# Identity by DMA, another order of the first loads, two weight loads ahead of the first gather, and one list operand on ScalarE

## The chip, the core and the metric

The kernel runs on one core of a Trainium2 chip. The metric is the device time of one execution in microseconds. The core has five engines that run side by side and in order, each through its own list of instructions: TensorE (PE, with its weight loads as PEld), VectorE (DVE), ScalarE (ACT), GpSimd (POOL) and SyncE (SP). DMA transfers are issued by an engine into a queue of its own and carried out by 16 DMA engines that all queues share. An instruction that has to wait for another engine, or for a transfer, waits at the head of its engine's list, and all behind it waits too.

## The reference, cut to what matters

```python
# attention in chunks of 64 tokens: q, k, v are (8, 8, 576, 64)
scores = scale * q_c @ k_c.T              # each chunk of 64 against itself
attn = exp(scores - max) ; attn /= sum + 1e-9
x = (attn @ v_c)  ->  (4608, 512)

# mixture of experts, 8 experts, a capacity of 576 tokens each
logits = x @ w_gate
for idx in argsort(-logits.flatten()):    # greedy: best logit first
    tok, e = idx // 8, idx % 8
    if not assigned[tok] and counts[e] < 576: assign
x[mask_e] = max(x[mask_e] @ w1[e], 0) @ w2[e]     # 512 -> 1024 -> 512

# a second block on all tokens
h = max(x @ m1, x @ m2, x @ m3)           # 512 -> 768
out = h @ w_out                           # 768 -> 512
```

All arrays are float32. The routing needs exact logits, and each expert gets exactly 576 tokens.

## The kernel before, in words

The program is written as one list for each engine; the order on an engine is the order of the code. There are three parts.

**Attention.** The 4608 tokens go in nine units of 512, each unit in four steps, 36 steps in all. A unit's k and q come with `load_qk` (lines 46 to 56), its v with `load_v` (lines 58 to 66: sixteen DMAs of 64 KB a unit, four for each of its four parts). PE turns k and q by transposes against an identity matrix (line 95), DVE and ACT copy the result out of PSUM into the block tiles kb and qT (`evac`, line 107), then come the scores (line 116), the softmax on DVE and ACT, a second transposing and the product with v (line 166). DVE scales the result into x (line 173, three buffers), and SP stores x to a DRAM array xd (line 175). The tiles kb and vb hold zeros in half of their blocks; these are set once by memsets at the start (lines 73 to 76). SP issues every load and store of this part; unit 0 and unit 1 are loaded ahead of the loop. The one exception is the gate weights wg, which ACT loads (line 83), after a memset of the tile on DVE (line 82).

The identity is made in `Router.__init__` (lines 278 to 284) by `make_identity`: POOL sets the tile to zero and then writes ones on the diagonal with an affine select.

**Routing and experts.** `Router.round` (lines 389 to 531) picks for one expert the 576 tokens it gets. It is a generator: the first round runs alone, the rounds for the later experts are stepped through while the expert before computes. At its end it makes the list of tokens. A comparison on DVE gives the tile `at` (line 503, 128 x 720), two multiplications give the two halves of an operand, `tok[:, 0]` by column (line 504) and `tok[:, 1]` by row (line 505), and 36 small matmuls add them up (line 511). DVE casts the sums into `ids` (line 514), PE folds them (line 520), and DVE casts the fold into the index `idx` (line 522).

With the index POOL gathers the expert's rows of xd in five indirect DMAs (line 614; 128 tokens each, 64 in the last). PE transposes the rows (line 637), ACT and DVE part them into a high and a low half (lines 639, 640), and the expert runs as two products (line 796 with ReLU at lines 805 and 813, then line 825); each operand is kept as a high and a low half, and every product is made of such halves. The copy of the result is ACT's (line 832), and ACT stores it too (line 833).

The expert weights come in chunks of 512 KB. `issue` (line 574) lets SP load one into one of four raw buffers; `split` (line 586) parts it, first a cast on ACT (line 594, the high half), then a subtraction on DVE (line 595, the low half). A counter sets the pace: `pump` (line 715) is called between the matmuls, steps the routing of the next expert, the weights of the last block (lines 677 to 709, with an `ACTIVATE` into ct at line 688) and, every second time, `pump_loads` (line 598), which splits the oldest chunk when it is old enough and issues another load. In the first round the loop at lines 728 to 731 issues loads while the list is made. After the gather's issue PE runs twelve matmuls without use (`warm`, line 732), two chunks are split, three row tiles are transposed, and SP stores one element of the last gathered tile to a DRAM cell `tick` (line 746): SP thus waits for the end of the gather before it issues more weights.

**The last block.** Lines 876 to 905 run over nine blocks of 512 tokens; nothing in it is touched.

What sets the order of issue on SP: a DMA's completion is counted on one of eight counters, given out in turn to the DMAs of SP and ACT in the order of the code, and a DMA is issued only after the one before it on the same counter has landed.

## Time and profile before

| | |
|---|---|
| median of three runs | 1318.49 us (1316.15 to 1322.0) |
| the profiled execution | 1317.84 us, its span in the trace 1316.1 us |
| PE busy | 1245.3 us (95%) |
| PE's weight loads | 1085.4 us (82%) |
| DVE busy | 663.9 us (50%) |
| ACT busy | 397.4 us (30%) |
| POOL busy | 108.5 us (8%) |

Busy is the time in which an engine carried out an instruction; time in which it waited or issued a DMA does not count. In the rows further down, a line like `L505 DVE ... aoh<-aoh,row` tells the line of the code, the engine, and what was made out of what, by the names of the tiles. Tiles that share a buffer share the first name it had: `aoh` stands for the operands of the list too, `rp` for the small results in PSUM, `pT` for the transposes of q and k, `raw` and `chunk` for an expert's weights before and after the parting. A name with a `q` behind an engine, such as SPq, is the engine's issuing side. The idle time in brackets is that of the engine just ahead of the instruction, with what ended it. PEclk is the mean clock that the chip granted TensorE, 1.00 for 2.4 GHz and 0.50 for 1.2 GHz.

### The profile page before, as it was taken

To read this page: it belongs to the slowest core of one execution; us is meant where nothing else is said; L and a number is where in the kernel's file an instruction comes from. 1 tells how busy PE (TensorE), PEld (TensorE's weight loads), DVE (VectorE), ACT (ScalarE), POOL (GpSimd) and SP (SyncE) were. 2 spreads that over 40 slices of the span, in tenths; PEclk is the share of its full clock that TensorE was granted. 3 is DMA by queue.
4 is the path that set the end of the run, shared out by engine and by line. 5 is a ranking of instruction groups with operands and counts; after the bars stand their busy time and mean duration, and the time that the engine had idled before them with its cause. 6 is when DMAs were issued, how large, how long until landed. Compare 5 with 4: busy or idle time off the path is not lost.

```text
span 1316.1 us, 20997 instructions
## 1 busy us (share of the span) xinstructions
PE 1245.3 (95%) x8669; PEld 1085.4 (82%) x8669; DVE 663.9 (50%) x1332; ACT 397.4 (30%) x621; POOL 108.5 (8%) x171
## 2 busy tenths in 40 slices
PE   5999975998999999999999999999999999999997
PEld 4877854988888988999999888888888888888885
DVE  5777876888787888795422422222222222222221
ACT  4877831332432323343323212121212121212110
POOL 6000001011010110110000000000000000000001
PEclk9999985999999999999999999999999999999998
DMA  8888724264553544567314101010101010100000
GB/s 196 215 223 226 222 76 132 65 228 138 156 173 108 166 139 134 183 216 236 104 65 171 60 17 49 17 48 16 48 20 45 25 41 24 40 24 9 24 9 32
DMA packets 147458, 135.60 MB, mean 103 GB/s; under 512 B 45731, under 2 KB 122531, under 8 KB 147363
## 3 DMA queue, kind: packets, MB, share of 16 engines
q1 hardware_dynamic: 136402, 105.93, 27.3%
q0 software_dynamic: 5824, 18.88, 4.2%
q10 hardware_dynamic: 5136, 9.46, 2.0%
q8 instruction: 68, 1.11, 0.4%
q14 instruction: 28, 0.22, 0.1%
HBM read 99.63 MB, written 34.60 MB: 102 GB/s over the span
## 4 chain that ended last, share of the span: by engine, by line
PE 39%; issue 35%; DVE 13%; DMA 6%; POOL 2%; ACT 2%; SPq 2%; POOLq 0%; ACTq 0%; DVEq 0%
PE acc L825 12%; PE acc L796 10%; PE acc L876 5%; DMA xd<-x 4%; PE pc L876 3%; DVE chunk L595 2%; PE po L899 2%; POOL out_dram L905 2%; DVE hlo L813 1%; PE pX L166 1%; SPq L64 1%; PE pS L116 1%; PE pT L95 1%; DVE ge L417 1%; PE pxt L637 1%
## 5 line engine op out<-in xcount | busy, mean ns | idle before, releaser
L825 PE MATMUL acc<-hhi,chunk 128*128 128x288 f32 x1024 | 214.7, 303 | 0.0
L796 PE MATMUL acc<-xhi,chunk 128*128 128x288 f32 x1024 | 210.9, 305 | 1.3 <-ACT xhi L639 0.7
L796 PEld LDWEIGHTS acc<-xhi,chunk 128*128 128x128 f32 x1024 | 162.8, 191 | 3.9 <-DVE hlo L813 1.3
L825 PEld LDWEIGHTS acc<-hhi,chunk 128*128 128x128 f32 x1024 | 164.1, 190 | 1.0
L885 DVE TENSOR_TENSOR tb<-ta,acc 128x512 f32<-128x512 f32 x54 | 37.1, 688 | 235.1 <-ACT ta L883 235.1
L825 PE MATMUL acc<-hlo,chunk 128*128 128x288 f32 x512 | 151.6, 296 | 0.1
L876 PE MATMUL acc<-yxhi,chunk 128*128 128x512 f32 x480 | 147.8, 389 | 0.0
L796 PE MATMUL acc<-xlo,chunk 128*128 128x288 f32 x512 | 144.4, 297 | 0.0
L876 PE MATMUL acc<-yodd,chunk 128*128 128x512 f32 x576 | 134.5, 389 | 0.0
L876 PEld LDWEIGHTS acc<-yodd,chunk 128*128 128x128 f32 x576 | 108.1, 188 | 22.5
L595 DVE TENSOR_TENSOR chunk<-raw,chunk 128x1024 fp32r<-128x1024 f32 x75 | 90.9, 1219 | 33.2 <-ACT chunk L594 33.2
L876 PEld LDWEIGHTS acc<-yxhi,chunk 128*128 128x128 f32 x480 | 90.0, 188 | 18.7
L825 PEld LDWEIGHTS acc<-hlo,chunk 128*128 128x128 f32 x512 | 96.9, 189 | 0.3 <-DVE hlo L813 0.3
L796 PEld LDWEIGHTS acc<-xlo,chunk 128*128 128x128 f32 x512 | 94.8, 190 | 0.0
L883 ACT COPY ta<-acc 128x512 f32<-128x512 f32 x54 | 31.7, 587 | 206.0 <-PE acc L876 203.9
L876 PE MATMUL acc<-yxlo,chunk 128*128 128x512 f32 x240 | 93.4, 389 | 0.0
L905 POOL DMA_INDIRECT out_dram<-ot,ia x36 | 34.7, 964 | 671.0 <-DVE ot L903 618.2
L805 ACT ACTIVATE hhi<-acc 128x576 fp32r<-128x576 f32 x64 | 41.8, 652 | 152.5 <-PE acc L796 152.5
L594 ACT CAST chunk<-raw 128x1024 fp32r<-128x1024 f32 x75 | 76.8, 1045 | 33.8 <-DMA raw<-in_moe_w_dram 26.1
L899 PE MATMUL po<-chunk,hm 128*128 128x512 f32 x324 | 79.3, 389 | 0.0
L886 DVE TENSOR_TENSOR tb<-tb,pc 128x512 f32<-128x512 f32 x54 | 37.1, 687 | 73.4 <-PE pc L876 73.4
L876 PE MATMUL pc<-yxhi,chunk 128*128 128x512 f32 x240 | 73.9, 389 | 0.0
(197 smaller groups left out, 1827.5 us busy)
## 6 DMA issues: line engine op xcount, KB each, us to landing
raw<-in_moe_w_dram SPq DMA_DIRECT2D x64, 512.0 KB, 5.3
vb<-in_v_dram SPq DMA_DIRECT2D x144, 64.0 KB, 3.6
xd<-x SPq DMA_DIRECT2D x36, 256.0 KB, 4.2
c<-in_moe_w_dram SPq DMA_DIRECT2D x36, 256.0 KB, 4.1
yd<-ys ACTq DMA_DIRECT2D x32, 288.0 KB, 3.5
yraw<-yd SPq DMA_DIRECT2D x9, 1024.0 KB, 5.0
m<-ct SPq DMA_DIRECT2D x36, 128.0 KB, 1.9
raw<-m SPq DMA_DIRECT2D x9, 512.0 KB, 3.7
```

Source lines behind the costliest of these rows:

```text
L64: nc.sync.dma_start(t[s * 64:(s + 1) * 64, j, :, s, :], bass.AP(tensor=v.tensor, offset=v.offset + b * H * S * D + s * S * D + c * 64 * D, ...
L594: nc.scalar.copy(hi, raw)
L595: nc.vector.tensor_tensor(lo, raw, hi.bitcast(F32), op=OP.subtract)
L796: nc.tensor.matmul(acc[:, hf, :288], w[a][:, dc, o:o + 128], x[:, dc, tk], start=n == 0, stop=n == 11)
L805: nc.scalar.activation(hv, acc[:, :, :288], AF.Relu)
L825: nc.tensor.matmul(acc[:, hf, :288], w[a][:, f, :], x[:, f, tk], start=n == 0, stop=n == 23)
L876: nc.tensor.matmul(ps, w[a][:, dc, o:o + 128], x[:, dc], start=n == 0, stop=n == 11)
L883: nc.scalar.copy(ta, pab[:, 0])
L885: nc.vector.tensor_tensor(tb, ta, pab[:, 1], op=OP.max)
L886: nc.vector.tensor_tensor(tb, tb, pc, op=OP.max)
L899: nc.tensor.matmul(po, h[:, x, t * 128:t * 128 + 128], w[a][:, f % 2], start=n == 0, stop=n == 17)
L905: st = nc.gpsimd.indirect_dma_start(out=out, out_offset=bass.IndirectOffsetOnAxis(ap=ia[:, 4 * b + t:4 * b + t + 1], axis=0), in_=ot, in_o ...
```

## The change

Four things are changed.

1. The identity. DVE sets the tile to zero and its column 0 to one. ACT stores this tile (128 x 128, 64 KB) to a DRAM array `unit` and reads it back with a pitch of 127 elements between rows and not 128, so that the one of row p comes to stand p places to the right. POOL no longer takes part.
2. The start. The memset and the load of wg are written ahead of the other memsets; the memsets of the first vb tile go from POOL to DVE; and unit 0's v and unit 1's k and q are loaded in turns (v part 0, k and q part 0 of unit 1, v parts 1 and 2, k and q part 1 of unit 1, v part 3) and no longer all of v first.
3. The list operand `tok[:, 1]` is made on ACT, as a copy with a scale for each partition, and no longer on DVE.
4. Two weight loads and not four are issued ahead of the first gather.

```diff
--- before.py
+++ after.py
@@ -4,7 +4,6 @@
 import concourse.tile as tile
 from concourse import mybir
 from concourse._compat import with_exitstack
-from concourse.masks import make_identity
 from concourse.bass_isa import ReduceOp
 
 F32 = mybir.dt.float32
@@ -68,19 +67,21 @@
 
     load_qk(0, 0)
     load_qk(0, 1)
+    wg = C.tile([128, 4, 32], F32, name="wg")
+    nc.vector.memset(wg, 0.0)
+    nc.scalar.dma_start(wg[:, :, :8], wg_in.rearrange("(a p) e -> p a e", p=128))
     VB = [C.tile([128, 8, 4, 2, 64], F32, name="vb%d" % i) for i in range(3)]
     KB = [C.tile([128, 8, 4, 2, 64], F32, name="kb%d" % i) for i in range(2)]
-    for t, eng in ((KB[0], nc.vector), (KB[1], nc.gpsimd), (VB[0], nc.gpsimd), (VB[1], nc.gpsimd),
+    for t, eng in ((KB[0], nc.vector), (VB[0], nc.vector), (KB[1], nc.gpsimd), (VB[1], nc.gpsimd),
                    (VB[2], nc.gpsimd)):
         eng.memset(t[0:64, :, :, 1, :], 0.0)
         eng.memset(t[64:128, :, :, 0, :], 0.0)
-    for part in range(4):
-        load_v(0, part)
+    load_v(0, 0)
     load_qk(1, 0)
+    load_v(0, 1)
+    load_v(0, 2)
     load_qk(1, 1)
-    wg = C.tile([128, 4, 32], F32, name="wg")
-    nc.vector.memset(wg, 0.0)
-    nc.scalar.dma_start(wg[:, :, :8], wg_in.rearrange("(a p) e -> p a e", p=128))
+    load_v(0, 3)
 
     def trans(nm, u, n):
 
@@ -275,13 +276,17 @@
 
 
 
-    def __init__(s, ctx, tc, mark):
+    def __init__(s, ctx, tc, mark, scratch):
         s.tc, s.mark = tc, mark
         nc = s.nc = tc.nc
         C = s.C = ctx.enter_context(tc.tile_pool(name="rc", bufs=1))
         s.L = C.tile([128, G, E], F32, name="L")
         s.ident = C.tile([128, 128], F32, name="ident")
-        make_identity(nc, s.ident)
+
+        nc.vector.memset(s.ident, 0.0)
+        nc.vector.memset(s.ident[:, 0:1], 1.0)
+        nc.scalar.dma_start(scratch, s.ident)
+        nc.scalar.dma_start(s.ident, bass.AP(tensor=scratch.tensor, offset=scratch.offset, ap=[[127, 128], [1, 128]]))
 
     def consts(s, tmp):
         nc, C = s.nc, s.C
@@ -502,7 +507,7 @@
 
         nc.vector.tensor_tensor(at, bb(qi, 20), s.i20[:, None, :].to_broadcast([128, G, 20]), op=OP.is_equal)
         nc.vector.tensor_tensor(tok[:, 0], at, s.col, op=OP.mult)
-        nc.vector.tensor_scalar(tok[:, 1], at, s.row, None, op0=OP.mult)
+        nc.scalar.activation(tok[:, 1], at, AF.Copy, scale=s.row)
         yield 3
         mark("r.list")
         pi = PS.tile([128, 2, 5, 4], F32, name="rp", tag="rp", bufs=2)
@@ -541,7 +546,8 @@
     yd = dram.tile([DM, NT], F32, name="yd")
     tick = dram.tile([1, 1], F32, name="tick")
     ms = [dram.tile([DM, F2], F32, name="m%d" % i) for i in range(3)] + [dram.tile([F2, DM], F32, name="mo")]
-    rt = Router(ctx, tc, mark)
+    unit = dram.tile([128, 128], F32, name="unit")
+    rt = Router(ctx, tc, mark, unit)
     with ExitStack() as c2:
         consts = c2.enter_context(tc.tile_pool(name="tmp", bufs=1))
         rt.consts(consts)
@@ -727,7 +733,7 @@
 
     rt.begin()
     for _ in rt.round(0, PS, expert):
-        if state["issued"] < 4:
+        if state["issued"] < 2:
             issue()
     def warm(n):
 
@@ -742,7 +748,6 @@
     split()
     for i in range(3):
         x_tr(0, xg, i)
-
     nc.sync.dma_start(tick, xg[4][0:1, 0:1])
 
     NB = NT // 512
```

On ACT, the first instructions of the program: before, the load of wg, the table load and the copies of the transposes (pT, out of PSUM).

```order
L947 UNCONDITIONAL_BRANCH [waits barrier_Pool_Activation_PE_DVE_SP_release]
L83 DMA wg<-in_moe_w_gate_dram 128x4x8 [waits DVE_49]
L107 ACT_TABLE_LOAD
L107 COPY kb_167<-pT 64x2x8x32 [waits PE_49]
L107 COPY qT<-pT 64x512 [waits PE_49]
```

```order
L952 UNCONDITIONAL_BRANCH [waits barrier_Pool_Activation_PE_DVE_SP_release]
L288 DMA unit<-ident 128x128 [waits DVE_49]
L289 DMA ident<-unit 128x128 [waits DMAHW1_49]
L72 DMA wg<-in_moe_w_gate_dram 128x4x8 [waits DVE_49]
L108 ACT_TABLE_LOAD
L108 COPY kb_171<-pT 64x2x8x32 [waits PE_49]
```

The store and the read of the identity now stand ahead of wg; the read waits for the store's landing (DMAHW1 is its counter), and wg and the copies stand behind that.

On SP, the first v loads of unit 0 and what follows them (DMAHW0 to DMAHW7 are the eight counters; before, wg's is DMAHW3; in the changed kernel the store of the identity has DMAHW1, its read DMAHW3 and wg DMAHW5). Before:

```order
L64 DMA vb_164<-in_v_dram 64x4x64 x3
L64 DMA vb_164<-in_v_dram 64x4x64 [waits DMAHW0_49]
L64 DMA vb_164<-in_v_dram 64x4x64 [waits DMAHW1_49]
L64 DMA vb_164<-in_v_dram 64x4x64 [waits DMAHW2_49]
L64 DMA vb_164<-in_v_dram 64x4x64 [waits DMAHW3_49]
L64 DMA vb_164<-in_v_dram 64x4x64 [waits DMAHW4_49]
```

```order
L63 DMA vb_168<-in_v_dram 64x4x64
L63 DMA vb_168<-in_v_dram 64x4x64 [waits DMAHW0_49]
L63 DMA vb_168<-in_v_dram 64x4x64 [waits DMAHW1_49]
L63 DMA vb_168<-in_v_dram 64x4x64 [waits DMAHW2_49]
L52 DMA ink<-in_k_dram 16x4x256 [waits DMAHW3_49]
L52 DMA ink<-in_k_dram 112x4x256 [waits DMAHW4_49]
L52 DMA inq<-in_q_dram 16x4x256 [waits DMAHW5_49]
L52 DMA inq<-in_q_dram 112x4x256 [waits DMAHW6_49]
L63 DMA vb_168<-in_v_dram 64x4x64 [waits DMAHW7_49]
```

After four v loads, and not sixteen, stand four loads of k and q of unit 1, the first of which waits for the read of the identity.

On SP, at the first gather (raw is a buffer of weights, tick the store that waits for the gathered tile xg). Before:

```order
L566 TENSOR_LOAD ei_141
L566 ISA x2
L581 ISA
L581 DMA raw_2999<-in_moe_w_dram 128x4x256
L581 ISA
L581 DMA raw_3016<-in_moe_w_dram 128x4x256
L581 ISA
L581 DMA raw_3021<-in_moe_w_dram 128x4x256
L581 ISA
L581 DMA raw_3062<-in_moe_w_dram 128x4x256
L746 DMA tick<-xg 1x1
```

```order
L572 TENSOR_LOAD ei_142
L572 ISA x2
L587 ISA
L587 DMA raw_3000<-in_moe_w_dram 128x4x256
L587 ISA
L587 DMA raw_3017<-in_moe_w_dram 128x4x256
L751 DMA tick<-xg 1x1
L587 ISA
L587 DMA raw_3163<-in_moe_w_dram 128x4x256
L587 ISA
L587 DMA raw_3177<-in_moe_w_dram 128x4x256
```

The third and the fourth load now stand behind tick, and so behind the end of the gather.

On ACT, at the list of round 5, which runs while the expert before it computes (aoh is the list operand, xhi the high half of gathered rows, ct a step of the last block's weights, ys and yd the copy and the store of a result). Before:

```order
L639 CAST xhi<-pxt 128x4x64
L688 ACTIVATE ct<-c_6117 128x512
L594 CAST chunk<-raw_6214 128x1024
L832 COPY ys<-acc 128x576
L833 DMA yd<-ys 128x576
L594 CAST chunk<-raw_6331 128x1024
```

```order
L645 CAST xhi<-pxt 128x4x64
L510 ACTIVATE aoh<-aoh,row 128x720
L694 ACTIVATE ct<-c_6118 128x512
L600 CAST chunk<-raw_6215 128x1024
L837 COPY ys<-acc 128x576
L838 DMA yd<-ys 128x576
L600 CAST chunk<-raw_6332 128x1024
```

The new step stands ahead of a ct step and of the cast of a chunk.

## Rows read from the trace of the kernel before

**Rows 1.** Windows: stretch, us, busy PE PEld DVE ACT POOL, clock, DMA share, GB/s.

```profile
600.00:1309.00 709.00, 707.07 (x3490) 604.43 (x3488) 191.14 (x267) 136.71 (x217) 37.90 (x73) 1.00 0.14 48
```

**Rows 2.** Timeline of the first 30 us: start, duration, instruction, idle time before it.

```profile
1.23 1.76 DVE L75 MEMSET kb<- 64x2048 f32 x1 [1.23 <-PEq L936]
...
5.49 0.43 ACTq L83 DMA_DIRECT2D wg<-in_moe_w_gate_dram  x1
...
10.27 0.28 POOL masks.py:199 TENSOR_SCALAR_AFFINE_SELECT ident<-ident 128x128 f32<-128x128 f32 x1 [9.32 <-issue]
...
10.60 1.12 PE L95 MATMUL pT<-ident,ink 128*128 128x128 f32 x4 [10.60 <-DMA vb<-in_v_dram]
...
12.41 0.69 DVE L107 COPY kb<-pT 64x512 f32<-64x512 f32 x1 [6.95 <-ACT kb L107]
```

**Rows 3.** SP's second k load; packets in 0:9.3, in 9.3:10.3; landings: wg, ink, vb.

```profile
1.79 0.51 SPq L53 DMA_DIRECT2D ink<-in_k_dram  x1
...
q1 hardware_dynamic: 2877, 2.28, 78.9%
...
q10 hardware_dynamic: 528, 0.02, 31.3%
...
wg<-in_moe_w_gate_dram ACTq DMA_DIRECT2D x1, 16.0 KB, 5.8
...
DMA to landing us min/median/max: 4.0/5.0/5.9
...
DMA to landing us min/median/max: 2.3/2.4/2.7
```

**Rows 4.** Timeline of SP's issues and DVE's first x; duration of a v issue (ns).

```profile
2.89 14.91 SPq L64 DMA_DIRECT2D vb<-in_v_dram  x16
...
29.84 0.69 DVE L173 TENSOR_TENSOR x<-pX,rc 128x512 f32<-128x512 f32 x1
...
36.69 0.42 SPq L175 DMA_DIRECT2D xd<-x  x1
...
L64 SPq DMA_DIRECT2D vb<-in_v_dram x16: 595/615/738, 2.9 to 17.2; - x16
```

**Rows 5.** SP's waits in 0:20 and 20:32: in total us, times, longest.

```profile
SPq L64 <- DMA wg<-in_moe_w_gate_dram: 2.9, 1, 2.9
...
SPq L64 <- DMA inq<-in_q_dram: 1.8, 2, 1.1
SPq L53 <- DMA ink<-in_k_dram: 0.8, 1, 0.8
```

**Rows 6.** The first gather's issues (ns, first and last start), landings, first expert matmul.

```profile
L614 POOL DMA_INDIRECT xg<-xd,idx x5: 912/947/1427, 213.0 to 218.8; - x5
...
DMA to landing us min/median/max: 3.2/3.9/5.9
...
222.41 1.81 PE L796 MATMUL acc<-xhi,chunk 128*128 128x288 f32 x6 [0.67 <-ACT xhi L639]
```

**Rows 7.** Windows after the first expert matmul and at round 6's list.

```profile
226.00:228.00 2.00, 2.00 (x12) 2.00 (x12) 1.93 (x5) 0.10 (x1) 0.00 (x0) 0.64 0.69 208
520.00:525.00 5.00, 5.00 (x45) 4.74 (x40) 4.79 (x14) 0.00 (x0) 0.00 (x0) 0.66 0.52 156
```

**Rows 8.** Line 505 over all rounds: ns min/median/max, first and last start.

```profile
L505 DVE TENSOR_SCALAR aoh<-aoh,row x8: 399/400/401, 210.7 to 539.7; 128x720 bf16<-128x720 bf16 x8
```

**Rows 9.** Timeline at round 5's list; its last row is round 6's list.

```profile
468.51 1.04 ACT L594 CAST chunk<-raw 128x1024 fp32r<-128x1024 f32 x1
...
471.91 0.53 DVE L504 TENSOR_TENSOR aoh<-aoh,col 128x720 bf16<-128x720 bf16 x1
...
472.68 1.22 DVE L595 TENSOR_TENSOR chunk<-raw,chunk 128x1024 fp32r<-128x1024 f32 x1
...
474.47 0.21 PE L520 MATMUL rp<-ids,lev 128*32 128x5 f16 x8
...
519.45 0.74 PE L511 MATMUL rp<-aoh 128*32 128x40 bf16 x36 [1.58 <-DVE aoh L505]
```

## The prediction

> **What bounds the kernel now.** I read the windows by stage first, then the timeline of the first 30 us, SP's own waits, the first gather, and last the timeline round one of the list steps. The kernel is a row of stages, and only what is late next in each stage counts.
>
> At the very start PE waits for the identity: POOL makes it at 10.27 and the first transposes start at 10.60; DVE's first copy follows at 12.41, because PE's second buffer waits for it [rows 2]. From then on the attention does not follow PE but SP, which issues every load and store. It needs 14.91 us for the sixteen v loads, and the store of the first x tile leaves at 36.69 although DVE had made the tile at 29.84 [rows 4]. SP is then behind for good, and x has three buffers, so DVE soon waits for SP's stores to land. What counts in this stage is when SP gets through its list, not when PE starts. SP's own waits name what holds it: 2.9 us for the gate weights, which ACT issues, and 1.8 + 0.8 us for the second unit's q and k [rows 5].
>
> At the first gather the chain is serial: the list, the gather on POOL, transposes, and the first expert matmul at 222.41 [rows 6]. Up to about 600 us PE and DVE work in step and wait for each other; from 600 on PE is busy 707 of 709 us [rows 1]. A loss of PE time before 600 therefore stays in the time.
>
> **The change, part by part.** The sum is made against the profiled run's 1317.84 us (span 1316.1, and 1.7 around it); the median of the three runs, 1318.49, is 0.65 above that.
>
> *The start.* The identity now needs two DMAs of 64 KB one after the other, both from ACT, whose queue stands still between them. DVE can fill the tile from 1.23 on, with two memsets of about 0.2 us, so the write is issued at about 1.6. Its price is read from the one ACT load of this stage: wg was issued at 5.49 [rows 2], its queue moved no packet up to 9.3 while SP's queue moved 2877, its 528 packets all went in 9.3 to 10.3, and it landed 5.8 us after issue [rows 3]. A DMA from ACT thus stood behind what SP had issued before it. The two k loads of the first unit land 4.0 and 5.9 us after their issue, the second, issued at 1.79, at 7.7 [rows 3]. The write is issued just ahead of that one and stands behind the first half of k and q alone, so it lands near 6.5; the read stands behind the rest of the first loads and two or three v loads, which as wg did clear after 10, and lands near 10.5. That is where POOL's identity was ready: PE gains nothing (0.1). Bounded from the other side, without a queue each costs the 2.3 us of an uncrowded v load [rows 3]: 1.6 + 2 x 2.3 = 6.2. PE could then start at 6.3, but DVE, with the two memsets of VB[0] added, does four memsets of 1.76 us [rows 2] and is free at about 9.2 and not before; against 12.41 this is at most 3.2 us.
>
> The Trainium skill says something else of this queue (*DMA: Bandwidth & Descriptors*, Queues, rings and completion order): each DMA engine takes turns between the queues that have work, packet by packet, so ACT's small DMAs would not stand behind SP's. The row on wg speaks against it here. By the page the start would be worth the 3.2 us, and the rival below would be the case.
>
> *SP's list.* Every issue on SP waits for the DMA eight places before it, and unit, ident and wg take three of these places. Four v loads are out when SP stops for the read of ident at 10.5 (before: six, and a stop for wg until 11.3). Twenty issues are left up to the loop: 12 of v at 0.65 (0.615 [rows 4] and a small gap) and 8 of q and k at 0.52 (0.51 [rows 3]), 12.0 us. They end at 22.5; before it was 14.91 + 2.89 = 17.8 [rows 4] and eight issues more, 22.0. So 0.5 us later. In exchange, half of the second unit's q and k (1 MB of 2) leaves in the quiet stretch at 10 to 13 us, and not in one burst at 18 to 22, behind which SP stood for 1.8 + 0.8 = 2.6 us [rows 5]. I take that wait as gone: 0.5 - 2.6 = **-2.1 us**. Bounds: +0.5 if the waits come back later, and -4.7 if ACT's DMAs do not queue (SP would be through at about 19.9: -2.1, and the same -2.6). Compute has the slack for it: it was 6.9 us ahead at the first store. The earlier VB[0] on DVE hides ahead of 12.41, POOL is done earlier with the others, and ACT's table load ends long before its first copy; these cost nothing as long as PE does not start before 9.
>
> *The gather.* Four weight loads of 512 KB leave ahead of it; POOL's five pieces start from 213.0 to 218.8, land 5.9 us (first) to 3.2 us (last) after issue, and take 1.43 us to issue at worst against 0.91 [rows 6]. With two loads the queue is empty by about 213, so the first piece should land in the 3.2 us of the last: at 216.2 and not 218.9, the others about every 1.25 us (the median issue of 0.95 and a gap of 0.3, by the five starts). Not all 2.7 us arrive: the third tile is then bound by POOL's pace (218.7), its transposes and copy end at 220.5, and the first expert matmul starts there and not at 222.41: **-1.9 us**. The other two loads now stand behind tick, which waits for the last piece (about 221), so they land near 225 to 227; their splits stand one step later on ACT and DVE and come at about 238, so nothing waits for them: 0, at most +0.5. What is open is the clock. In 226 to 228 the grant is 0.64 on the mean [rows 7], that is, it rises from 1.2 to 2.4 GHz in there, some 5 us after the first expert matmul, with an idle stretch of PE ahead of the transposes. If the closed gap lets it rise right away, the 5 us at half clock are done in half: -2.5 more.
>
> *The list operand.* Each of eight rounds takes 0.40 us off DVE [rows 8] and puts the same tile on ACT, where a cast of 1024 columns takes 1.04 us [rows 9]; 720 columns are 0.73 of that by columns, and I take 0.78. ACT can start when L503 ends and is done 0.8 us later; on DVE the pair L504 and L505 (0.53 and 0.40 us) took about 0.9 [rows 8, 9]. The list matmuls start 0.1 us earlier at most, where ACT is free. But ACT runs in order, and the new step waits for DVE. Whatever stands behind it on ACT waits as well. In round 5 that is a ct step and the cast of a chunk. The cast ran at 468.51, 3.4 us ahead of L503's end (L504 starts at 471.91) [rows 9]. Now it comes after list (to 472.69) and ct (to 473.3) and ends at 474.2. DVE's second half of that split, which started at 472.68 [rows 9], starts at 474.25, and behind it on DVE stands ids, for which PE's fold at 474.47 [rows 9] waits: ids comes at 475.6, PE stops for 1.1 us, and everything behind it. The same reading gives 0.4 in round 4, 0.5 in round 6, 1.2 in round 7; in rounds 1 to 3 no split stands between, and 0.1 each is won. 3.2 - 0.3 = **+2.9 us**, bounds -0.3 (the casts are not waited for) and +6.3 (clock, below). The 0.40 us that DVE is spared each round does not count further, as its next wait for PE takes it up.
>
> Sum: -2.1 - 1.9 + 2.9 = -1.1, 1317.84 - 1.1 = **1316.7 us**.
>
> **The rivals.**
> (a) *ACT's DMAs take turns with SP's.* The identity lands near 6.3, wg near 8, and SP is through early: -4.7 in place of -2.1, so -3.7, 1314.1 us. For it: the trace shows ACT's queue in this stage with one DMA only. Against it: that one stood for 3.8 us [rows 2, 3].
> (b) *The list operand on ACT hurts nobody*, because the splits of rounds 4 to 7 have slack that I don't see: -0.3 for +2.9, so -4.3, 1313.5 us. Against it: DVE and PE stand back to back there [rows 9].
> (c) *The clock rises with the closed gap at the gather*: -4.4 for -1.9, so -3.6, 1314.2 us.
> (d) *Slower: the stall on ACT costs the clock too.* In round 6 PE stood 1.58 us ahead of the list [rows 9], and 520 to 525 has a mean grant of 0.66 [rows 7]. With 1.1 to 1.2 us more of standing in rounds 5 and 7, the grant could fall twice; such a fall cost half of some 3.4 us there (0.34 of 5 us at 0.50 is 1.7 us of work). 2 x 1.7 = 3.4 more: +2.3, 1320.1 us. It decides once PE's stop in these rounds is longer than the one of round 6.
> (e) *SP's list gains nothing* (the burst's waits come back, or ident lands after 12): +0.5 for -2.1: +1.5, 1319.3 us.
>
> **How the numbers follow.** Forecast 0.30, (a) 0.18, (b) 0.17, (c) 0.10, (d) 0.13, (e) 0.12. The cases are not exclusive: (a) with (b), or (b) with (c), gives -6.8 or -6.9, 1311.0, and (d) with (e) +4.9, 1322.7. The range reaches from the first of these to 1321.5, which leaves out less than 2 in 10. About 0.5% (6.6 us) is what a measurement of this kernel can tell from no change. Only two of the good cases together reach it: faster 0.14. On the bad side (d), (e) and a worse gather would all have to come: slower 0.03. Same 0.83.
>
> **What would show it.** Right, if the first transposes start between 10 and 11 us and the read of ident lands just before; if SP has no wait over 0.5 us between 22 and 32 us and the first x store leaves near 34.5; if the first piece of the gather lands 3.2 us after its issue and the first expert matmul follows the gather's issue by 7.5 us (before 9.4); if in rounds 5 and 7 ACT's cast of a chunk comes after the new step, and PE's fold waits for ids by about 1 us. Wrong, if PE starts before 9 us (a), if the fold starts on time (b), if the grant is 1.0 before 222 us (c), or if short stretches at half clock follow rounds 5 and 7 (d).

## The result, and the profile after

The changed kernel takes 1332.84 us (median of six runs, 1328.22 to 1335.68) against 1318.0 us (six runs of the kernel before, 1315.97 to 1322.0): a ratio of 1.0107, with a 95% interval of 1.0081 to 1.0133. It is 14.8 us slower by the medians, where I had forecast 1316.7 us and no difference that can be measured. The ratio is not the quotient of the two medians, which is 1.0113; by the ratio the difference is 14.1 us. The profiled execution took 1335.68 us with a span of 1333.9, the longest of the six, so it shows some 3 us more than the median.

To see where the time went I set the same DVE instruction of both traces side by side, all through the program, and took the difference of their starts. The first column is the time in the kernel before; positive means that the changed kernel is late.

| time in before, us | what stands there | changed kernel late by, us |
|---|---|---|
| 26 | attention, unit 1 begins | -1.9 |
| 46 | attention | +0.1 |
| 205 | first list | +0.7 |
| 222.4 | first expert matmul | 0.0 |
| 241 | first expert, fifth part of its first product | -1.7 |
| 247 | 6 us on | +3.4 |
| 257.5 | | +6.8 |
| 347 | expert 2 | +8.7 |
| 475 | list of round 5 | +10.9 |
| 545 | list of round 7 | +15.6 |
| 600 to the end | | +17.8 |

From 600 us on nothing changes any more. The window that answers to [rows 1], 17.8 us later, is the same to a tenth; the second row is the stretch behind the first loss, the third the one behind round 5's list (columns as in [rows 1]: length, busy time of PE, PEld, DVE, ACT, POOL, then the granted clock).

```profile
617.80:1326.80 709.00, 707.10 (x3490) 604.47 (x3488) 191.16 (x267) 136.69 (x217) 37.72 (x71) 1.00 0.14 48
250.00:256.90 6.90, 6.33 (x29) 6.02 (x29) 4.04 (x11) 0.65 (x1) 0.00 (x0) 0.51 0.01 2
485.60:489.00 3.40, 3.40 (x15) 3.40 (x15) 3.11 (x11) 0.34 (x1) 2.30 (x3) 0.50 0.71 236
```

**The start.** The timeline of the changed kernel (start, duration, engine and line), answering to [rows 2, 4]:

```profile
1.16 0.41 ACTq L288 DMA_DIRECT2D unit<-ident  x1
5.07 0.34 ACTq L289 DMA_DIRECT2D ident<-unit  x1
...
8.32 1.76 DVE L78 MEMSET vb<- 64x2048 f32 x1 [0.47 <-issue]
...
11.12 1.08 PE L96 MATMUL pT<-ident,ink 128*128 128x128 f32 x4 [11.12 <-DMA vb<-in_v_dram]
...
35.93 0.42 SPq L176 DMA_DIRECT2D xd<-x  x1
```

And SP's waits in 0 to 20 us and in 20 to 32 us, answering to [rows 5] (engine, line, what it waited for: us in total, times, longest):

```profile
SPq L52 <- DMA ident<-unit: 3.8, 1, 3.8
...
SPq L63 <- DMA inq<-in_q_dram: 0.9, 1, 0.9
```

The identity is there at 11 us, not earlier than POOL had it (10.55). DVE is through with its memsets at 10.08 us, where the prediction's bound had 9.2. SP stands 3.8 us for the identity's read, and in return the wait of 2.6 us for the second unit's q and k is down to 0.9.

**The first gather**, answering to [rows 6]: POOL's issues with their landings, and the first expert matmul in PE's timeline.

```profile
L620 POOL DMA_INDIRECT xg<-xd,idx x5: 915/947/1424, 214.0 to 219.8; - x5
...
DMA to landing us min/median/max: 3.1/3.3/3.7
```

```profile
222.41 1.81 PE L801 MATMUL acc<-xhi,chunk 128*128 128x288 f32 x6 [0.68 <-ACT xhi L645]
```

The pieces land sooner after their issue, 3.7 us at most where it was 5.9; but the gather begins 1.0 us later (0.7 us of this from the attention, 0.3 from the list), and the first expert matmul comes at 222.41 in both kernels.

**The first loss, 240 to 257 us.** ACT, DVE and PE of the changed kernel, one after the other:

```profile
239.62 1.98 ACT L600 CAST chunk<-raw 128x1024 fp32r<-128x1024 f32 x2
243.56 0.65 ACT L810 ACTIVATE hhi<-acc 128x576 fp32r<-128x576 f32 x1 [1.96 <-PE acc L801]
247.57 0.66 ACT L694 ACTIVATE ct<-c 128x512 f32<-128x512 f32 x1 [3.35 <-DMA c<-in_moe_w_dram]
248.13 1.03 ACT L600 CAST chunk<-raw 128x1024 fp32r<-128x1024 f32 x1
...
249.19 1.23 DVE L601 TENSOR_TENSOR chunk<-raw,chunk 128x1024 fp32r<-128x1024 f32 x1 [3.36 <-ACT chunk L600]
250.33 0.18 DVE L439 TENSOR_TENSOR cs<-rp,same 128x32 f16<-128x32 f32 x1
...
250.57 0.25 PE L444 MATMUL rp<-cs,lev 128*32 128x8 f16 x4 [4.35 <-DVE cs L439]
```

The same place in the kernel before, ACT and PE:

```profile
240.21 1.98 ACT L594 CAST chunk<-raw 128x1024 fp32r<-128x1024 f32 x2
244.51 0.65 ACT L805 ACTIVATE hhi<-acc 128x576 fp32r<-128x576 f32 x1 [2.32 <-PE acc L796]
247.18 0.66 ACT L688 ACTIVATE ct<-c 128x512 f32<-128x512 f32 x1 [2.02 <-DMA c<-in_moe_w_dram]
...
247.17 0.24 PE L439 MATMUL rp<-cs,lev 128*32 128x8 f16 x4
```

In both kernels ACT comes to a ct step (a step of the last block's weights) and waits for its load c, 2.02 us before and 3.35 us after. In the kernel before the four casts of this stretch, those of the third to the sixth chunk, are done by then, and nobody waits for ACT. In the changed kernel the two loads behind tick have put every split one step later; the fourth cast, that of the sixth chunk, stands behind the ct step, DVE waits 3.36 us for it, cs (a small step of the next expert's routing) waits behind it on DVE, and PE waits 4.35 us for cs. Then the granted clock stands at 0.51 for 6.9 us (the second window above).

**The later losses.** Round 5's list in the changed kernel, ACT, DVE and PE, answering to [rows 9]:

```profile
481.55 0.89 ACT L510 ACTIVATE aoh<-aoh,row 128x720 bf16<-128x720 bf16 x1 [3.87 <-DVE aoh L508]
482.35 0.68 ACT L694 ACTIVATE ct<-c 128x512 f32<-128x512 f32 x1
482.94 1.03 ACT L600 CAST chunk<-raw 128x1024 fp32r<-128x1024 f32 x1
...
484.00 1.23 DVE L601 TENSOR_TENSOR chunk<-raw,chunk 128x1024 fp32r<-128x1024 f32 x1 [1.91 <-ACT chunk L600]
485.14 0.19 DVE L519 CAST ids<-rp 128x40 f16<-128x40 f32 x1
...
485.39 0.22 PE L525 MATMUL rp<-ids,lev 128*32 128x5 f16 x8 [1.17 <-DVE ids L519]
```

This is the order that I had worked out: list operand, ct step, cast, and behind it DVE's subtraction and ids, for which PE's fold waits 1.17 us. In rounds 4, 5, 6 and 7 PE waits 0.60, 1.17, 0.43 and 1.18 us there, 3.4 in all. At rounds 5, 6 and 7 the clock falls to half: the third window above and these two, 13.6 us in all.

```profile
533.30:540.10 6.80, 6.37 (x35) 6.09 (x34) 6.05 (x18) 1.05 (x3) 0.00 (x0) 0.50 0.32 96
557.20:560.60 3.40, 3.18 (x20) 3.16 (x20) 3.26 (x9) 0.78 (x1) 0.00 (x0) 0.51 0.24 87
```

The kernel before has one such stretch there, at round 6:

```profile
521.00:524.40 3.40, 3.40 (x23) 3.22 (x22) 3.23 (x11) 0.00 (x0) 0.00 (x0) 0.50 0.45 133
```

Not every fall belongs to a stop that the edits made. The changed kernel's trace has two more of 3.4 us, from 328.5 and 349.0 us, with none of these stops ahead of them, and the trace of a kernel without the new list operand (start_alone below) has such a fall at 307.6 us too.

### The profile page after: what moved, and what is told of

Read it like the earlier page. It is cut to its first block, busy times and chain, and to the rows that moved or that the text cites. A ratio compares the mean times of both kernels' runs of the same rounds, so it can differ in the third digit from the quotient of the medians.

```text
span 1333.9 us, 21005 instructions
## 1 busy us (share of the span) xinstructions
PE 1253.2 (94%) x8669; PEld 1093.1 (82%) x8669; DVE 666.0 (50%) x1328; ACT 403.6 (30%) x629; POOL 104.3 (8%) x167
## 4 chain that ended last, share of the span: by engine, by line
PE 38%; issue 34%; DVE 12%; DMA 8%; ACT 3%; POOL 3%; SPq 1%; POOLq 0%; ACTq 0%; DVEq 0%
PE acc L830 11%; PE acc L801 9%; PE acc L881 5%; DMA xd<-x 3%; PE pc L881 3%; DVE chunk L601 3%; PE po L904 2%; POOL out_dram L910 2%; PE pX L167 2%; PE pT L96 1%; DMA c<-in_moe_w_dram 1%; PE pS L117 1%; DVE hlo L818 1%; DMA vb<-in_v_dram 1%; DVE ge L422 1%
## 5 line engine op out<-in xcount | busy, mean ns | idle before, releaser
L830 PE MATMUL acc<-hhi,chunk 128*128 128x288 f32 x1024 | 217.9, 306 | 0.0
L801 PE MATMUL acc<-xhi,chunk 128*128 128x288 f32 x1024 | 215.5, 310 | 2.1 <-DVE hlo L818 1.5
L801 PEld LDWEIGHTS acc<-xhi,chunk 128*128 128x128 f32 x1024 | 166.6, 195 | 4.7 <-DVE hlo L818 2.2
L830 PEld LDWEIGHTS acc<-hhi,chunk 128*128 128x128 f32 x1024 | 166.9, 193 | 1.1
```

Of the source, the lines that this page charges most:

```text
L801: nc.tensor.matmul(acc[:, hf, :288], w[a][:, dc, o:o + 128], x[:, dc, tk], start=n == 0, stop=n == 11)
L830: nc.tensor.matmul(acc[:, hf, :288], w[a][:, f, :], x[:, f, tk], start=n == 0, stop=n == 23)
```

## The experiments

All ratios are against runs of the kernel before on the same chip. The runs come in three sets on three chips, in which the kernel before takes 1318.82, 1319.04 and 1320.67 us, so ratios and not times are to be held against each other. A ratio can differ from the quotient of the two medians by up to 0.0008, which is 1 us. "Time at half clock" is an estimate from each run's span and mean granted clock, 2 x (1 - clock) x span, and is a mean over a kernel's runs. In the first set (two_alone, two_count, list_alone, start_alone) the kernel before has 54.0 us of it; the changed kernel, in its own six runs, 64.3.

### Two loads alone

```diff
-        if state["issued"] < 4:
+        if state["issued"] < 2:
```

> The kernel before with two loads and not four ahead of the first gather, and nothing else. Theory (head of line on ACT): the first piece of the gather lands 3.5 us after issue and not 5.9, the first expert matmul comes at 221 to 222, and then the first expert loses what it lost in the changed kernel: a ct step on ACT that waits for its load stands ahead of a chunk cast, DVE and PE stand for 3 to 4 us near 247, the clock falls to half behind it. Time 6 to 8 us above before, 1324 to 1326 us. Rival 1 (the loss in the first expert comes from the other edits, by chance of their timing): 1316 to 1318 us, no stop over 1 us in 222 to 265. Rival 2 (my prediction's term): 1316 us.

Measured: 1326.95 us against 1318.82, ratio 1.0061 (1.0043 to 1.0079). This one edit costs 8.1 us, the upper end of what the theory said. The ct step and the matmul that waits for cs in its trace:

```profile
250.22 0.66 ACT L688 ACTIVATE ct<-c 128x512 f32<-128x512 f32 x1 [3.20 <-DMA c<-in_moe_w_dram]
...
253.22 0.24 PE L439 MATMUL rp<-cs,lev 128*32 128x8 f16 x4 [4.20 <-DVE cs L434]
```

It is the stop of the changed kernel again, 4.20 us here. Time at half clock is 61.9 us, 7.9 more than in the kernel before; if half of that is lost, 4.2 + 4.0 = 8.2 us. This is an estimate, and the trace confirms only a part of it: behind the stop it has 3.4 us at half clock, which cost 1.7.

```profile
253.60:257.00 3.40, 3.40 (x15) 3.11 (x15) 1.95 (x6) 0.65 (x1) 0.00 (x0) 0.50 0.02 5
```

The first expert matmul comes at 224.6 us and not at the 221 to 222 that I expected; the attention of this run was already 2.9 us behind the trace of the kernel before at 205 us.

### Two loads, and the casts where they were

```diff
-            inflight.append([raw, -3 if state["issued"] % 8 == 0 else 0])
+            inflight.append([raw, -3 if state["issued"] % 8 == 0 else 1 if 2 <= state["issued"] < 6 else 0])
```

beside the edit of two_alone.

> Two loads ahead of the first gather as in two_alone, but the counters of the next four chunks start one higher, so that the order of all instructions on ACT, DVE and PE is that of the kernel before; only the two loads come later (landing near 227 and 228 and not 215 and 217). Theory (the order of casts behind ct is what costs): the stop near 247 is gone, the first expert runs as in before, and what the lighter gather wins stays: 1316 to 1318 us. Rival (the chunks themselves come too late for their casts): the loss of the first expert stays, 1324 to 1326 us, and casts wait for raw's landing between 226 and 240.

Measured: 1317.11 us, ratio 0.9989 (0.9975 to 1.0002). ACT's ct step and PE's matmul at the same place:

```profile
248.31 0.66 ACT L688 ACTIVATE ct<-c 128x512 f32<-128x512 f32 x1 [2.28 <-DMA c<-in_moe_w_dram]
...
248.05 0.24 PE L439 MATMUL rp<-cs,lev 128*32 128x8 f16 x4
```

The ct step waits as before, but PE no longer does. The loads are as late as in two_alone, so their lateness costs nothing that can be measured; the order of the splits costs the 8 us. The rival falls. Which of the four casts it is, the run best further down tells.

### Two loads, casts late, but the ct step's load early

```diff
         load(jobs[0])
         yield
+        yield
@@
-        if state["idx"] == E - 1:
+        if state["idx"] == E - 1 or state["pump"] == 8:
             next(converting, None)
```

beside the edit of two_alone.

> Two loads ahead of the first gather, casts in the late order of two_alone, but the load of the first ct step is issued ten pumps earlier, so that the step no longer waits for it on ACT. Theory (not the late cast as such costs, but that it stands behind a ct step that waits for its load): the 4.2 us stop of PE near 253 shrinks to 1 us or less; time 1318 to 1321 us. Rival (the late order costs by itself, since DVE's list of work is then full in the wrong place): a stop of over 2.5 us stays, 1324 to 1327 us.

Measured: 1321.88 us against 1319.04 in this set, ratio 1.0026 (1.0005 to 1.0047). This lies between the theory's range and the rival's.

```profile
245.58 0.67 ACT L689 ACTIVATE ct<-c 128x512 f32<-128x512 f32 x1
...
248.60 0.24 PE L439 MATMUL rp<-cs,lev 128*32 128x8 f16 x4 [0.90 <-DVE cs L434]
```

With c there in time the stop is 0.90 us and not 4.2. So most of the stop is the ct step's wait for its load, passed on through ACT's order, and not the late cast as such. About 3 us of loss stay (0.7 to 6.2 by the interval). The late chunk's subtraction, 1.22 us on DVE from 247.22 us, still stands right ahead of cs; the rest of the 3 us is not explained.

### The list operand alone

```diff
-        nc.vector.tensor_scalar(tok[:, 1], at, s.row, None, op0=OP.mult)
+        nc.scalar.activation(tok[:, 1], at, AF.Copy, scale=s.row)
```

> The kernel before with the list operand on ACT, and nothing else. Theory: PE's fold waits for ids by 0.4 to 0.6 us in rounds 4 and 6 and by 1.1 to 1.2 us in rounds 5 and 7, 3.3 us in all, and a fall of the granted clock follows in two or three of these rounds, 1.7 us each: 1322 to 1327 us. Rival 1 (the stops alone, no clock): 1321 us. Rival 2 (in the changed kernel the rounds were late for another reason): 1317 to 1318 us, no stop of PE at the fold over 0.3 us.

Measured: 1326.42 us, ratio 1.0058 (1.0042 to 1.0073). PE's idle time ahead of the fold, us and times, in the kernel before and then in this one:

```profile
  DVE ids L514: 0.3, 1
```

```profile
  DVE ids L514: 3.2, 4
```

The stops are there, 0.59, 1.16 and 1.18 us in rounds 4, 5 and 7 (the 0.3 of round 0 are in both). Their sum, 2.9, is less than half of the loss. Time at half clock is 60.9 us against 54.0: half of the 6.9 us is 3.5, and 2.9 + 3.5 with 0.25 us in round 0, where the list matmuls begin later, makes 6.7 of the 7.6. The profiled run of this kernel was its fastest (1323.31 us) and shows two falls of the clock in the experts' part, where the trace of the kernel before has three; none stands right behind a fold. Round 5's fold is at 476.82 us, and the clock stays up behind it:

```profile
476.00:480.00 4.00, 3.18 (x31) 3.16 (x31) 3.47 (x13) 1.05 (x1) 2.05 (x2) 1.00 0.76 251
```

So the clock's share rests on the mean over the runs alone, and no trace of this kernel shows it.

### The list operand with PE kept busy

As list_alone, and ahead of the fold:

```diff
-        pf = PS.tile([128, 5], F32, name="rp", tag="rp", bufs=2)
+        pf = PS.tile([128, 512], F32, name="rp", tag="rp", bufs=2)
+        if r in (5, 7):
+            for _ in range(6):
+                nc.tensor.matmul(pf[:, :384], s.ones, s.i32.rearrange("p a c -> p (a c)")[:, :384], start=True, stop=True)
+        pf = pf[:, :5]
```

> list_alone with six matmuls without use (384 columns each) ahead of PE's fold in rounds 5 and 7, so that PE works through most of the 1.2 us for which it stood there. Theory (part of the loss of list_alone is the clock, which falls after such stops): the wait for ids shrinks to 0.2 to 0.4 us, the mean time at half clock falls from 61 to 55 or 57 us a run, and the time by 2 to 3 us, 1323 to 1324.5 us. Rival (the clock falls for other reasons, and its difference in list_alone was chance): time and time at half clock as in list_alone, 1326 us and 61 us.

Measured: 1325.0 us against 1320.67 in this set, ratio 1.0033 (1.0016 to 1.0051). PE's idle time ahead of the fold:

```profile
  DVE ids L514: 1.8, 5
```

What is left are 0.30 us in round 0 and 0.57 and 0.59 in rounds 4 and 6, which are not filled; rounds 5 and 7 have under 0.2. Time at half clock is 59.3 us against 55.9 of the kernel before in this set, 3.4 more and not 6.9. The ratio falls from 1.0058 to 1.0033, though the filling matmuls take PE's time instead of the stop and give back no work. This speaks for the clock as the other half. But the two intervals overlap (from 1.0042 to 1.0051), and both the time and the time at half clock came out above what the theory said, so the clock's share is likely and not shown.

### The list operand later in ACT's list

```diff
-        nc.vector.tensor_scalar(tok[:, 1], at, s.row, None, op0=OP.mult)
         yield 3
+        nc.scalar.activation(tok[:, 1], at, AF.Copy, scale=s.row)
```

> The list operand on ACT as in list_alone, but written three pumps later, right ahead of the list matmuls, so that the chunk cast stands ahead of it on ACT. Theory (head of line): PE's fold no longer waits for ids in rounds 4, 5 and 7 (0.6, 1.2 and 1.2 us before); instead the list matmuls wait for ACT, which in these rounds comes to the operand only after a copy of a result: 0.3 to 0.6 us more in each. 1319 to 1322 us. Rival (ACT is too slow for the step wherever it stands, 0.90 us against 0.40 on DVE): as list_alone, 1325 to 1327 us.

Measured: 1320.72 us against 1319.04, ratio 1.0008 (0.9988 to 1.0028). PE's idle time ahead of the fold, and ahead of the list matmuls:

```profile
  DVE ids L514: 0.3, 1
...
  ACT aoh L506: 12.2, 8
```

The fold waits for nothing again. The list matmuls wait 12.2 us in all, where list_alone has 11.0 and the kernel before 10.4. The same step on the same engine, behind the cast and not ahead of it, costs 1.1 us by the ratio, which cannot be told from nothing, and not 7.6. The rival falls.

### The list operand on ACT in rounds 0 to 3 alone

```diff
-        nc.vector.tensor_scalar(tok[:, 1], at, s.row, None, op0=OP.mult)
+        if r < 4:
+            nc.scalar.activation(tok[:, 1], at, AF.Copy, scale=s.row)
+        else:
+            nc.vector.tensor_scalar(tok[:, 1], at, s.row, None, op0=OP.mult)
```

> The list operand on ACT in rounds 0 to 3 alone, where no cast of a chunk stands behind it within the next steps (in round 0 two casts do, before PE has anything to do), on DVE in rounds 4 to 7. Theory: round 0 costs 0.3 us in the serial chain, rounds 1 to 3 nothing; 1318.5 to 1320 us, and no stop of PE at the fold. Rival (every round on ACT costs the same, 7.6 / 8): 1322 to 1323 us.

Measured: 1320.22 us, ratio 1.0004 (0.9983 to 1.0025), and at the fold no stop but the 0.3 us of round 0 that the kernel before has too. Rounds 0 to 3 cost nothing that can be measured; the loss of list_alone is thus that of rounds 4 to 7, where a cast stands behind.

### The start alone, and its two parts

start_alone is the changed kernel with the list operand on DVE and four loads. order_alone has besides the identity made by POOL again; ident_alone is the kernel before with the identity by DMA and nothing else.

> The changed kernel with the list operand back on DVE and four loads ahead of the first gather, so that the identity by DMA and the order of the first loads alone are left. Theory (from 40 us on the attention follows what the DMA engines carry, whatever the start gains): 1.5 to 2 us ahead at 25 us, nothing of it at 46 us, 0 to 0.8 us behind at 205 us; time 1317.5 to 1319 us, the same as before. Rival (the gain stays where the rest is not in its way, and the changed kernel lost it only by its other edits): 1315.5 to 1316.5 us, with the last softmax of the attention 1.5 us earlier than in before.

> The new order of the first loads (wg first, v and unit 1's k and q in turns, first vb memsets on DVE) with the identity still made by POOL, list operand on DVE, four loads. Theory (my step: what counts is SP's list, not the identity): as start_alone, 3 to 4 us ahead of typical runs of before at 25 us and 1.5 us at 205; 1317 to 1318 us. Rival (the identity by DMA is what gains): as before, 1319 us.

> The kernel before with the identity by DMA alone. Theory: the read of the identity stands in the queues behind SP's loads, PE starts at 10.5 to 12 us as before, wg comes no earlier: no gain, 1318.5 to 1320 us. Rival (the start's gain is the identity's): 1317 to 1318 us, PE's first transposes before 9 us.

Measured: start_alone 1317.42 us, ratio 0.9983 (0.9968 to 0.9998); order_alone 1314.57 us, ratio 0.9948 (0.9931 to 0.9964); ident_alone 1322.79 us, ratio 1.0008 (0.999 to 1.0026). The new order wins 0.5%, and with the identity by DMA beside it more than half of this is gone. order_alone is faster than both kernels of this case. It holds three edits (wg first, the memsets on DVE, the turns of the loads), which no run parts. start_alone and order_alone come from two sets; in the set of order_alone the run best2 (below, with the start of start_alone) has 0.9975, so the identity by DMA costs 3 to 5 us there. On the old order it costs nothing clear: ident_alone's interval holds 1.

My theory for start_alone, that nothing of its gain is left at 46 us, does not hold: by the same comparison of starts as above, its trace is 2.1 us ahead of the kernel before at 26 us, 1.4 at 46 and 1.3 at 205.

What the old order costs is seen in a run that has it; two_alone has the same start as the kernel before. PE in two_alone at 20 to 28 us:

```profile
22.77 0.63 PE L95 MATMUL pT<-ident,ink 128*128 128x128 f32 x4 [1.70 <-DMA ink<-in_k_dram]
...
25.54 1.09 PE L95 MATMUL pT<-ident,inq 128*128 128x128 f32 x4 [2.14 <-issue]
```

and the window of 17 to 32 us, first in two_alone, then in order_alone:

```profile
17.00:32.00 15.00, 10.07 (x70) 7.78 (x72) 8.01 (x11) 6.00 (x11) 14.49 (x17) 0.77 0.99 214
```

```profile
17.00:32.00 15.00, 13.10 (x146) 10.82 (x147) 13.06 (x22) 10.49 (x18) 12.89 (x16) 1.00 0.88 195
```

In the old order PE waits 1.70 us for the second unit's k, then 2.14 us ahead of the transposes of q, for which this profile names no releaser (in late3 it names the load of q, 1.50 us), and the mean clock is 0.77; in order_alone neither happens. The other traces bear this out with one limit: of the nine with the old order of loads, eight have a fall of the clock in this window and all have a stop of 1.3 us or more; of the five with the new order none has a stop of 1 us, but best and best2 have a mean clock of 0.89. The profiled run that I predicted from is the one of the nine without a fall, with one stop of 1.36 us, so it showed less of this than the others. The seven later traces with the same start as before are 1.4 to 2.2 us behind it at 26 us.

SP's issues in order_alone say what the identity by DMA takes away:

```profile
3.04 2.91 SPq L64 DMA_DIRECT2D vb<-in_v_dram  x4
6.00 1.07 SPq L53 DMA_DIRECT2D ink<-in_k_dram  x2
...
33.41 0.43 SPq L177 DMA_DIRECT2D xd<-x  x1
```

The second unit's k leaves at 6.00 us; in the changed kernel SP stands until 11.0 for the read of the identity ahead of it. PE's first transposes come at 10.37 and not 11.12, and the first x store leaves at 33.41 and not 35.93. In the profiles order_alone is 2.5 us ahead of the kernel before at 205 us, start_alone 1.3. One trace of each is too few here: the profiled run of order_alone is the slowest of its ten (1317.92 us), and the four traces with the start of start_alone (it, the changed kernel, best and best2) lie from 1.3 us ahead to 1.7 behind at 205 us, 0.6 behind in the mean. Against that mean order_alone is 3.1 us ahead, about the 3 to 5 us between the times. So the identity's cost most likely arises in the attention, which SP's stop delays, but with one trace of order_alone this is not shown.

### All that does not cost, together

best and best2 are start_alone with two loads and raised counters.

> The changed kernel without what costs: identity by DMA and new order of the first loads, two loads ahead of the first gather with the order of casts of the kernel before (as two_count), list operand on DVE. If the two gains add (1.4 and 1.7 by the medians): 1315 to 1316.5 us. Rival (the lighter gather is worth nothing, since with four loads too the first expert matmul comes 8.6 to 8.8 us after the gather's issue in two of three traces): as start_alone, 1317.4 us.

In best the counters of three chunks were raised, not of the four that two_count had. Measured: 1324.12 us, ratio 1.004 (1.002 to 1.006).

```profile
247.97 0.66 ACT L694 ACTIVATE ct<-c 128x512 f32<-128x512 f32 x1 [2.72 <-DMA c<-in_moe_w_dram]
...
250.97 0.25 PE L444 MATMUL rp<-cs,lev 128*32 128x8 f16 x4 [3.72 <-DVE cs L439]
```

So it did not test what I meant it to, and tells something else: three of the four casts in their place do not help. The one behind the ct step costs it nearly all, as best2 shows, in which it too is in its place.

> As best, but with the counters of four chunks raised and not of three (in best the fourth cast still stood behind the ct step): now ACT and DVE have the order of the kernel before in the first expert. Theory: the 3.7 us stop near 251 is gone; the start's gain remains, the lighter gather adds nothing: 1316 to 1318 us. Rival (a stop remains there because the chunks land later): 1321 us or more.

Measured: 1317.95 us against 1320.67, ratio 0.9975 (0.9958 to 0.9993), no stop at that place. Against start_alone's 0.9983 the two loads add nothing that can be seen.

## Why the prediction was wrong, point by point

**Taken one by one the parts add up:** two loads +8.1 us, list operand +7.6, start -1.4, in sum +14.3; measured +14.8. By the ratios it is 8.0 + 7.6 - 2.2 = 13.4 against 14.1.

**"so nothing waits for them: 0, at most +0.5"** is the step that failed. I had seen that the splits of the third and fourth chunk move one step on ACT and DVE, and asked whether the chunks would be there in time and whether PE would need them. They were there: they landed at 226.8 and 228.2 us and were cast from 236.15 on. I followed these two alone, though the fifth and the sixth chunk stand behind them in the same list of splits and move along, and I did not ask what a moved cast would now stand behind. For the sixth chunk it was a ct step that waits 2 to 3.4 us for its load, a wait that was plain in the trace of before (2.02 us) and cost nothing there. I had named this very mechanism for the list operand, and did not apply it to a step that only changed places. Price: 8 us, shown by two_alone, two_count and two_early_c.

**The list operand, +2.9** was right in its mechanism and in its places: 0.4, 1.1, 0.5 and 1.2 us foreseen for rounds 4 to 7 (3.2 in sum), 0.60, 1.17, 0.43 and 1.18 found. The term was too small, 7.6 us measured, above its bound of 6.3. Two things were mis-sized. The step takes 0.895 us on ACT and not 0.78:

```profile
L510 ACT ACTIVATE aoh<-aoh,row x8: 894/895/896, 211.2 to 553.6; 128x720 bf16<-128x720 bf16 x8
```

so the list matmuls begin 0.04 to 0.1 us later in rounds 1 to 7 and 0.25 later in round 0, where I had 0.1 earlier. The Trainium skill (*ScalarE: Activation LUTs*, What ACT_TABLE_LOAD costs) gives about 280 ns and 0.833 ns a column for a step with one operand for each partition; an estimate from that is 0.88 us for 720 columns, and the trace agrees, 0.895 us. The larger part is likely the clock: rival (d) priced it, and I gave it 0.13 because I held the stops against the single longest stop of round 6. By the time at half clock it is about half of the loss, an estimate that list_fill supports and does not prove. Rival (b), no harm, is out.

**The gather, -1.9,** came to about 0.6 by the means of the traces, and to nothing that the times show (two_count 0.9975 to 1.0002; best2 against start_alone). With two loads the first transposes follow the gather's issue by 3.6 to 3.7 us in all six traces, with four by 4.3 to 7.2 in eight. But the first expert matmul follows by 8.2 to 8.8 us with two loads (mean 8.5) and by 8.5 to 10.7 with four (mean 9.2; five of the eight lie at 8.5 to 8.8). I had let POOL issue every piece in 1.25 us when the queue is empty; its first two still take 1.30 and 1.42 us, and the third tile sets the start. [Rows 6] was also one of the slower cases. Rival (c), the clock, did not come: behind the first expert matmul it stands at half speed as before.

```profile
222.40:226.20 3.80, 3.79 (x16) 3.32 (x17) 1.16 (x2) 0.96 (x2) 0.00 (x0) 0.51 0.45 133
```

**The start, -2.1,** held in kind: the identity comes at 11.0 us (10.5 foreseen), PE gains nothing, and SP's 2.6 us of waits in 20 to 32 us go down to 0.9. In size start_alone is 1.4 us faster by the medians and 2.2 by the ratio, but that this is near -2.1 is in part luck. In the changed kernel's trace the first x store leaves at 35.93, 0.8 us earlier and not 2.2, and what that trace had won at 26 us was gone at 46; the gain shows against other runs of the kernel before, which lose more at the start than the one that I summed from. My rival (a) is out: an identity at 6 us was not to be had. On the rule of the Trainium skill that I set against it (*DMA: Bandwidth & Descriptors*, Queues, rings and completion order) that each DMA engine takes turns between the queues that have work, the trace is divided. The store of the identity landed within 3.9 us of its issue, sooner than I had it behind the first loads. Its read took 5.9 us, as wg's load had taken 5.8, and from 5.1 to 7 us ACT's queue moved no packet while SP's moved 706. What I had not seen is that the two halves pull against each other: the new order wins, and the identity by DMA takes a part of it back, since SP waits for its read.

## What to carry to other kernels

When an edit moves a step in the order of an engine, look up what it now stands behind, and above all whether that waits for a DMA: a wait that costs nothing is free only as long as nothing that is needed stands behind it. Ask this of steps that merely come one place later, not only of new ones. And where PE is the bound, count a stop at more than its length, as the clock may fall behind it (here stops of 4.2 us cost 8.1 and stops of 2.9 us 7.6); and take a figure such as the time from the gather's issue to the first transposes from several traces where they are to be had, since the single profile showed 5.9 us for what is 4.3 to 7.2 with four loads.

## What the runs showed of the hardware that I had not expected

- A stop of 4.35 us of PE in the middle of dense work was followed by 6.9 us at a granted clock of 0.51 in the changed kernel, one of 4.20 us by 3.4 us at 0.50 in two_alone. Behind stops of 1.2 us the clock fell in one profile (485.6 us, 0.50 for 3.4 us) and not in another of the same order (list_alone, round 5, 1.00): it is not the same from run to run.
- The same multiplication of 128 x 720 bf16 elements takes 0.40 us on DVE and 0.895 on ACT.
- A gather's piece takes POOL 1.3 to 1.43 us to issue for the first two and 0.91 to 0.95 for the others, with two or with four weight loads in the queue.
